# Second products of two more groups as seven products of sums, block 0's result summed in the output by transfers, and weights paced by a modelled clock

## The chip, the cores and the metric

The kernel runs on one core of a Trainium2 chip. Its engines work side by side, each in its own order: TensorE (PE, matmuls; PEld is its loading of weights), VectorE (DVE), ScalarE (ACT), GpSimd (POOL) and SyncE (SP, which here only issues transfers). The metric is the device time of one execution in microseconds, lower is better. The kernel before was timed in three runs, and one more execution was profiled.

## The reference, cut to what matters

```python
x = retention(q, k, v)                      # [1536, 512], 2 sequences of 768, 8 heads of 64
xn = x / sqrt(mean(x * x) + 1e-6) * rms_g
x2 = (silu(xn @ w_gate) * (xn @ w_val)) @ w_out     # layer 1: 512 -> 1536 -> 512
h  = x2 @ w_in                                      # layer 2: 512 -> 2048 -> 512
out = maximum(0.01 * h, h) @ w_out2
```

The weights arrive as 64-bit floats. Every product is made of three float32r matmuls (high x high, high x low, low x high), so each operand has a high part (a ScalarE copy into float32r) and a low part (a VectorE difference).

## The kernel before

The 1536 tokens are three blocks of 512 (0, 1, 2). The hidden units are cut into blocks of 128: 12 in layer 1, 16 in layer 2. Four of these make a group: groups 0 to 2 are layer 1, groups 3 to 6 are layer 2. A group first makes its *first products* (g and v, or i) and then its *second products* (o, or p), which are summed over the four hidden blocks of the group in four PSUM banks and then added to a sum over groups in SBUF.

**First products.** Block 0 is computed plainly: `whole`, 12 matmuls of 128x512. Blocks 1 and 2, for a pair of hidden blocks, are made by `quad` as seven products of sums (the Strassen-Winograd scheme) of 6 matmuls each, in the order p1, p2, p6, p5, p7, p3, p4; p6, p5, p7 and p4 read T2, T1, T3 and T4, sums of the activations of blocks 1 and 2 that `sums_of` prepares once for each layer. At the border of the layers they are made from the last result of layer 1: VectorE sums (L773), ScalarE high parts (L776), VectorE low parts (L779).

**Second products.** `down` (12 matmuls) handles one hidden block and one token block. In the groups of `seven` (with `SEVEN = 2`: groups 5 and 6) only block 0 goes through `down`; blocks 1 and 2 go through `seventh`, seven products of sums for each pair of hidden blocks. That takes sums of pairs of weights p (L415, with parts L418 and L422, names w_sp), differences of activations in `follow` (L671), seven high and low parts for a pair instead of four, and after each of the seven products two additions of results (L722). `seventh` turns the result, so block 1 and 2 of layer 2 are kept turned in `y2` and turned back at the end. In these groups the second products of block 0 come one group later, between the first products.

**Weights.** A weight of 128x512 is fetched by SP as 64-bit words (three places, tag raw), taken apart by ScalarE (`prepare`, two copies), put together on VectorE (two small and two full-size operations: L456, L460, L465, L474), and split into a high part (ScalarE, L477) and a low part (VectorE, L481). The pieces are steps in the list `converting`. Finished weights lie in 14 places (12 of tag u, 2 of units2) until their last product.

**Order.** The start (all of the retention) follows an order written out by hand. Then `run` goes through the list of products that `plan` made: after each product it emits high parts of the next activations, up to two entries of `sums`, then `RATE` = 4 conversion steps for a full product (8 when behind, half for a half product), then low parts. `need` forces the conversion of a weight that is not there. The framework's scheduler may still move an instruction ahead of one that waits: the order on an engine is not always the program's.

**Result.** `evac2` copies (group 3, ScalarE, L743) or adds (groups 4 to 6, VectorE, L745) the four banks into `y2`, and in the last group sends block 0's rows out.

```python
        if gi in seven:
            for f in fs[::2]:
                own = [fill.pop(0) for _ in range(2)]
                for i7, (keys, step) in enumerate(quad("i", f)):
                    put(keys, step)
                    if i7 in BEHIND[2] and own:
                        own.pop(0)()
            wholes = [...]
            for n, more in zip((1, 5, 6, 3, 7, 2, 4), (1, 0, 1, 0, 1, 0, 1)):
                for f in fs[::2]:
                    ...   # seventh(gi, n, f)
                if more:
                    wholes.pop(0)()
```

Of the kernel before, what the change touches and what calls it, by code (L numbers as in the profile page):

```python
# [27 lines left out]
RATE = 4.0  # L28
TWICE = "gvi"
SEVEN = 2  # L30
# [29 lines left out]
def chain_kernel(ctx: ExitStack, tc: tile.TileContext, qk_t, kv, w1, w2, mask, qdec, kdec, sdec, rms_g, ident, out):  # L60
# [427 lines left out]
    def queue(unit):  # L488
        key, after, ops = unit
        take = lambda names: [ops.pop(n) for n in names if n in ops]  # L490
        if key in index and dict(wq)[key] is None:
            converting.extend(tails + take("123H4h"))
            tails[:] = take("Ll")
            return
        converting.extend(take("P12"))
        if after is not None and ("P" in opened_units[after][2] if after in opened_units else True):
            converting.append(lambda: prepare(after))
        converting.extend(tails + take("34H"))
        tails[:] = take("L")
# [29 lines left out]

    def convert(n=1):  # L530
        for _ in range(n):
            if not converting and not start_unit():
                converting.extend(tails)
                tails.clear()
                if not converting:
                    return
            converting.pop(0)()

    def need(key):
        while key not in wt:  # L540
            if not converting and not start_unit():
                assert tails
                converting.extend(tails)
                tails.clear()
            converting.pop(0)()
# [41 lines left out]
    def upper(key):  # L587
        if key in made:
            x = made.pop(key)
            h = gp.tile([P, 512], F32R, tag="gh", name="g{}_{}_{}h".format(*key))  # L590
            nc.scalar.activation(out=h, in_=x, func=AF.Copy)
            halves[key] = x, h

    def lower(key):
        if key in halves:
            x, h = halves.pop(key)
            l = gp.tile([P, 512], F32R, tag="gl", name="g{}_{}_{}l".format(*key))
            nc.vector.tensor_tensor(out=l, in0=x, in1=h.bitcast(F32), op=ALU.subtract)
            parted[key] = h, l
            if key[0] == "q":  # L600
                follow(key[1], key[2])

# [20 lines left out]
    def evac1(gi, b, banks):  # L623
# [13 lines left out]
        if last:  # L637
            def high(m):
                nc.scalar.activation(out=x2h[b][:, m, :], in_=acc[b][:, m, :], func=AF.Copy)

            def low(m):
                nc.vector.tensor_tensor(
                    out=x2l[b][:, m, :], in0=acc[b][:, m, :], in1=x2h[b][:, m, :].bitcast(F32), op=ALU.subtract
                )

            for do in (high, low):
                sums.extend([lambda m=m, do=do: do(m) for m in own])
            if b == 2:
                one, two = slice(0, 2), slice(2, 4)
                sums.extend(in_pairs(sums_of(acc, x2h, x2l, acc[1][:, one], acc[1][:, two], x2h[2][:, one], x2l[2][:, one])))  # L650
# [14 lines left out]
    turns = {}  # L665

# [19 lines left out]
    def seventh(gi, n, f):  # L686
        fs = groups[gi][1]
        key = ("q", f, n)
        if n == 1 and f == fs[0]:
            gather(gi)  # L690
        upper(key)
# [31 lines left out]
        if gi == len(groups) - 1 and LAST[b, row] == n:  # L723
            t = units.tile([P, 2, 16, 32], F32, tag="u", name=f"turned{b}_{row}")
            for m in range(2):
                nc.vector.transpose(
                    out=t[:, m], in_=y2[b][:, 2 * row + m, :].rearrange("p (j r) -> p j r", r=32)
                )
                for i in range(4):
                    o = (2 * row + m) * P + i * 32  # L730
                    nc.sync.dma_start(
                        out=out[offs[b]:offs[b] + 512, o:o + 32].rearrange("(j r) d -> r j d", r=32),
                        in_=t[32 * i:32 * i + 32, m],
                    )

    def evac2(gi, b, banks):
        first, last = gi == len(G1), gi == len(groups) - 1
        if first:
            y2[b] = xp.tile([P, 4, 512], F32, tag=f"acc{b}", name=f"y2acc{b}")
        for m in range(4):  # L740
            dst = y2[b][:, m, :]
            if first:
                nc.scalar.activation(out=dst, in_=banks[m], func=AF.Copy)  # L743
            else:
                nc.vector.tensor_tensor(out=dst, in0=banks[m], in1=dst, op=ALU.add)  # L745
            if last:
                r0 = offs[b] + m * P
                nc.sync.dma_start(out=out[r0:r0 + P, :], in_=dst)
# [5 lines left out]
    def sums_of(x, xh, xl, t1, t4, h1, l1):  # L754
# [58 lines left out]
    def place(n, key, own=None):  # L813

        if n == "v":
            return gates.pop(key)
        return scratch(f"{n}{key[0]}_{key[1]}") if own is None else own
# [23 lines left out]

    def whole(n, f, b, h, l):
# [3 lines left out]
        consume(n, f, b)  # L846
# [13 lines left out]
    def quad(n, f):  # L860
# [5 lines left out]
        def kept_sum(m, src):  # L866
            q[m] = scratch(f"{n}{m}_{f}")
            nc.scalar.activation(out=q[m], in_=src, func=AF.Copy)

        def added(key, src, m):  # L870
            t = q.pop(m)
            a = place(n, key, t)
            mid = t if n == "v" else a
            nc.vector.tensor_tensor(out=mid, in0=src, in1=t, op=ALU.add)
            use[n](key, mid, a)
# [33 lines left out]
        def p4():  # L909
            half(q["X"], own[1], True, "T4", False)  # L910
            use[n]((e, 1), q["X"], place(n, (e, 1)))
# [5 lines left out]
    def plan():  # L917
# [12 lines left out]
        for gi, (kinds, fs) in enumerate(groups):  # L930
# [18 lines left out]
            first = gi == len(G1)  # L949
            if gi in seven:  # L950
                for f in fs[::2]:
                    own = [fill.pop(0) for _ in range(2)]
# [4 lines left out]
                wholes = [lambda f=f: put((f"i{f}",), lambda: whole("i", f, 0, h, l)) for f in fs]  # L957
                for n, more in zip((1, 5, 6, 3, 7, 2, 4), (1, 0, 1, 0, 1, 0, 1)):
# [4 lines left out]
                    if more:  # L963
                        wholes.pop(0)()
                continue
            if first:

                for f, d in zip(fs, fill):
                    d()
                    put((f"i{f}",), lambda f=f: whole("i", f, 0, x2h, x2l))  # L970
# [134 lines left out]
    owed = 0.0  # L1105
# [12 lines left out]

    for i, (keys, b, step) in enumerate(steps[FIXED:], FIXED):
        ahead = max([index[k] for ks, _, _ in steps[i + 1:i + 4] for k in ks[:1] if k in index], default=0)  # L1120
        run(i, keys, b, step, RATE if started[0] > ahead else 2 * RATE)
# [69 lines left out]
```

## Time and profile before

| what | value |
|---|---|
| median of three runs | 587.68 us (587.67 to 588.03) |
| profiled execution, its own time | 587.79 us |
| span of the profiled execution | 586.0 us |
| TensorE, VectorE, ScalarE, GpSimd busy | 577.4, 480.8, 343.9, 19.3 us |
| granted TensorE clock, mean | 1.000 |

The span runs from the first to the last instruction; the execution's own time is 1.8 us longer. Busy time counts the time in which an engine has at least one instruction at work. Matmuls overlap: one is listed at 389 ns, but twelve of them take 2.72 us. VectorE's instructions overlap a little at their ends too.

### The profile page before, as it was taken

Reading aid. Unit: us, or ns where it says so; the run is one execution under the profiler, and the core shown is the slowest. Engines: PE = TensorE matmul, PEld = TensorE weight load, DVE = VectorE, ACT = ScalarE, POOL = GpSimd, SP = SyncE. Lnnn points to the kernel's source line nnn. Section 1 sums busy time; section 2 is a strip of 40 time slices with the busy share of each in tenths; the row PEclk is TensorE's granted clock in tenths of the full one; section 3 lists DMA queues with packets and bytes.
Section 4 is the critical chain, followed back from the end, with each engine's and each line's share of the span. In section 5 each row is a group of like instructions: output and inputs, shape, how many; then the busy total and the mean of one; then the engine's idle time right before and its main releaser. Section 6 shows DMA issues by size and latency. Waiting matters only on the chain.

```text
span 586.0 us, 8323 instructions
## 1 busy us (share of the span) xinstructions
PE 577.4 (99%) x3131; PEld 476.3 (81%) x3131; DVE 480.8 (82%) x865; ACT 343.9 (59%) x624; POOL 19.3 (3%) x20
## 2 busy tenths in 40 slices
PE   8899999999999999999999999999999999999997
PEld 6788788888888888888888888888888888888885
DVE  5899999999768589598598988874777679997893
ACT  2789656777655455365574666876653564574430
POOL 2332100000000000000000000000000000000000
PEclk9999999999999999999999999999999999999999
DMA  8991240534223023123230220422211010210055
GB/s 335 407 390 44 73 143 1 155 98 115 66 78 108 31 72 108 37 73 110 70 107 1 70 76 0 144 72 73 72 37 36 30 43 3 70 37 0 1 89 127
DMA packets 31769, 52.77 MB, mean 90 GB/s; under 512 B 18929, under 2 KB 19057, under 8 KB 31729
## 3 DMA queue, kind: packets, MB, share of 16 engines
q1 hardware_dynamic: 31584, 52.24, 27.7%
q8 instruction: 24, 0.39, 0.3%
q14 instruction: 17, 0.13, 0.1%
q10 hardware_dynamic: 144, 0.00, 0.0%
HBM read 49.09 MB, written 3.15 MB: 89 GB/s over the span
## 4 chain that ended last, share of the span: by engine, by line
PE 87%; DMA 6%; DVE 3%; ACT 2%; issue 1%; SPq 0%; POOLq 0%; DVEq 0%; ACTq 0%
PE ao L583 17%; PE ap L583 15%; PE iX L855 7%; PE i L554 7%; PE v L554 6%; PE g L554 6%; PE vX L855 5%; PE gX L855 5%; PE X L703 4%; PE iZ L855 4%; PE Z L703 3%; PE vZ L855 2%; PE gZ L855 2%; DMA qkv<-in_qk_t 2%; PE iY L855 2%; DMA qkv<-in_kv 2%
## 5 line engine op out<-in xcount | busy, mean ns | idle before, releaser
L583 PE MATMUL ap<-w_p,gp_0h 128*128 128x512 f32 x128 | 39.4, 389 | 0.0
L554 PE MATMUL g<-xh,w_g 128*128 128x512 f32 x128 | 31.8, 390 | 0.0
L554 PE MATMUL v<-xh,w_v 128*128 128x512 f32 x128 | 31.7, 390 | 0.0
L554 PE MATMUL i<-x2h,w_i 128*128 128x512 f32 x128 | 31.6, 389 | 0.0
L583 PE MATMUL ao<-go_2h,w_o 128*128 128x512 f32 x96 | 31.5, 389 | 0.0
L583 PE MATMUL ao<-go_0h,w_o 128*128 128x512 f32 x96 | 31.5, 389 | 0.0
L583 PE MATMUL ao<-go_1h,w_o 128*128 128x512 f32 x96 | 30.5, 389 | 0.0
L554 PEld LDWEIGHTS g<-xh,w_g 128*128 128x128 f32 x128 | 23.9, 188 | 5.2 <-issue 0.2
L583 PEld LDWEIGHTS ap<-w_p,gp_0h 128*128 128x128 f32 x128 | 24.0, 188 | 5.0
L554 PEld LDWEIGHTS i<-x2h,w_i 128*128 128x128 f32 x128 | 24.0, 188 | 5.0
L554 PEld LDWEIGHTS v<-xh,w_v 128*128 128x128 f32 x128 | 23.9, 188 | 5.0
L583 PE MATMUL ap<-w_p,gp_0l 128*128 128x512 f32 x64 | 24.9, 389 | 0.0
L583 PEld LDWEIGHTS ao<-go_2h,w_o 128*128 128x128 f32 x96 | 18.0, 188 | 3.7
L583 PEld LDWEIGHTS ao<-go_1h,w_o 128*128 128x128 f32 x96 | 18.0, 188 | 3.7
L583 PEld LDWEIGHTS ao<-go_0h,w_o 128*128 128x128 f32 x96 | 18.0, 188 | 3.7
L583 PE MATMUL ap<-gp_2h,w_p 128*128 128x512 f32 x64 | 21.0, 389 | 0.0
L798 ACT ACTIVATE i<-i 128x512 f32<-128x512 f32 x16 | 9.6, 597 | 18.8 <-PE i L554 18.8
L583 PE MATMUL ap<-gp_1h,w_p 128*128 128x512 f32 x64 | 20.5, 389 | 0.0
L855 PE MATMUL iX<-th,w_si 128*128 128x512 f32 x64 | 19.7, 390 | 0.0
L855 PE MATMUL iZ<-x2h,w_si 128*128 128x512 f32 x64 | 19.7, 389 | 0.0
L583 PE MATMUL ao<-go_0l,w_o 128*128 128x512 f32 x48 | 18.7, 389 | 0.0
L583 PE MATMUL ao<-go_1l,w_o 128*128 128x512 f32 x48 | 18.7, 389 | 0.0
(303 smaller groups left out, 1662.7 us busy)
## 6 DMA issues: line engine op xcount, KB each, us to landing
raw_i<-in_w SPq DMA_DIRECT2D x16, 512.0 KB, 3.7
raw_p<-in_w SPq DMA_DIRECT2D x16, 512.0 KB, 3.6
raw_g<-in_w SPq DMA_DIRECT2D x12, 512.0 KB, 3.7
raw_v<-in_w SPq DMA_DIRECT2D x12, 512.0 KB, 3.7
raw_o<-in_w SPq DMA_DIRECT2D x12, 512.0 KB, 4.2
qkT<-in_qk_t SPq DMA_DIRECT2D x7, 512.0 KB, 6.5
kv<-in_kv SPq DMA_DIRECT2D x7, 512.0 KB, 8.0
qkv<-in_qk_t SPq DMA_DIRECT2D x5, 512.0 KB, 11.0
```

The lines of the kernel that those rows point to most:

```text
L554: nc.tensor.matmul(out=dst, lhsT=lhs, rhs=rhs, start=(n == 0), stop=(n == len(pairs) - 1), skip_group_check=True)
L583: nc.tensor.matmul(out=acc["b"][m], lhsT=lhs, rhs=rhs, start=(start and n == 0), stop=(stop and n == 2))
L703: nc.tensor.matmul(out=acc[side][m], lhsT=lhs, rhs=rhs, start=(start and f == fs[0] and k == 0), stop=(f == fs[-2] and k == 2), skip_group ...
L798: nc.scalar.activation(out=a, in_=x, func=AF.Prelu, alpha=0.01)
L855: nc.tensor.matmul(out=dst, lhsT=lhs, rhs=rhs, start=(start and n == 0), stop=(n == 5), skip_group_check=True)
```

## The change

`SEVEN` becomes 4: all four groups of layer 2 make the second products of blocks 1 and 2 by `seventh`. So the weights p of groups 3 and 4 are summed in pairs as well, and their activations are taken through `follow`.

Block 0's sum no longer lies in SBUF. In group 3 `evac2` copies the banks (ScalarE) into a tile `more` and SP writes it to the output; in groups 4 and 5 it is copied likewise and a transfer on POOL's queue adds it to the output in memory; in group 6 `recall` reads the output back into the tiles of raw weights, VectorE adds the last banks, and SP writes the rows. `more` lies where block 0's layer 1 sum was. It also holds block 0's activations of the first products (`place`), and at the border T2 for a while (`spare`), and the order of T1 to T4 and their parts changes.

At the border the plan begins with four `down`, then block 0's first product 0 (`HEAD`), and then the `quad`s follow; the other three products of block 0 come among the `seventh`s.

In `run` the low parts now follow the high parts directly. Conversion steps are emitted as long as each fits, by costs written in the code, below a modelled clock of TensorE (1.5 us more when behind); and the evacuations of a product (`later`) come after them, in `flush`. Results that are first in their place are copied by ScalarE (`fresh`).

```diff
-RATE = 4.0
-SEVEN = 2
+HEAD = "dddd0"
+OVER = 1.5
+COST = {n: ("a", 1.2) if n == "P" else ("a", 0.54) if n == "H" else ("v", 0.34 if n in "12" else 0.6) for n in "P1234HL"}
+COST_SUM = {n: ("a", 0.54) if n in "Hh" else ("v", 0.34 if n in "1234" else 0.6) for n in "123H4hLl"}
+SEVEN = 4
...
+    def convert_next():
+        key, engine, cost, do = converting.pop(0)
+        do()
+        done[key] = spend(engine, cost, done.get(key, 0.0))
...
         if f == fs[-1]:
-            (evac1 if L == "o" else evac2)(gi, b, acc.pop("b"))
+            banks = acc.pop("b")
+            first = gi in (0, len(G1))
+            by_copy = first or L == "p" and b == 0 and gi < len(groups) - 1
+            later.append(("a" if by_copy else "v", 2.4, lambda: (evac1 if L == "o" else evac2)(gi, b, banks)))
...
-            for do in (high, low):
-                sums.extend([lambda m=m, do=do: do(m) for m in own])
+            highs, lows = ([lambda m=m, do=do: do(m) for m in own] for do in (high, low))
             if b == 2:
                 one, two = slice(0, 2), slice(2, 4)
-                sums.extend(in_pairs(sums_of(acc, x2h, x2l, acc[1][:, one], acc[1][:, two], x2h[2][:, one], x2l[2][:, one])))
+                ops = sums_of(
+                    acc, x2h, x2l, acc[1][:, one], acc[1][:, two], x2h[2][:, one], x2l[2][:, one], extra()[:, two]
+                )
+                first_of = [lambda i=i: [ops[n]() for n in (f"{i}", f"h{i}")] for i in range(4)]
+                sums.extend(first_of[:2] + [ops["l1"]] + highs + [ops["l0"]] + lows)
+                sums.extend([first_of[2], ops["l2"], first_of[3], ops["l3"]])
+            else:
+                sums.extend(highs + lows)
...
+        if n == 5 and f == fs[0] and gi == len(groups) - 1:
+            recall()
...
-        for m in range(2):
-            dst = y2[b][:, 2 * row + m, :]
-            nc.vector.tensor_tensor(out=dst, in0=acc[side][m], in1=dst, op=ALU.add)
+        fresh = gi == len(G1) and (b, row) not in touched
+        touched.add((b, row))
...
+                if fresh:
+                    nc.scalar.activation(out=dst, in_=banks[m], func=AF.Copy)
+                else:
+                    nc.vector.tensor_tensor(out=dst, in0=banks[m], in1=dst, op=ALU.add)
...
         for m in range(4):
+            dst = y2[b][:, m, :] if b else more[0][:, m, :]
+            rows = out[offs[b] + m * P:offs[b] + (m + 1) * P, :]
+            if b and not first:
+                nc.vector.tensor_tensor(out=dst, in0=banks[m], in1=dst, op=ALU.add)
+            elif last:
+                nc.vector.tensor_tensor(out=partial[m], in0=banks[m], in1=partial[m], op=ALU.add)
+                nc.sync.dma_start(out=rows, in_=partial[m])
+            else:
                 nc.scalar.activation(out=dst, in_=banks[m], func=AF.Copy)
+                if not b and first:
+                    nc.sync.dma_start(out=rows, in_=dst)
+                elif not b:
+                    nc.gpsimd.dma_start(out=rows, in_=dst, accum_op=ALU.add)
...
+    def recall():
+        for m in range(0, 4, 2):
+            t = raws.tile([P, 2, 512], F32, tag="raw", name=f"partial{m}")
+            for k in range(2):
+                partial[m + k] = t[:, k]
+                nc.sync.dma_start(out=t[:, k], in_=out[offs[0] + (m + k) * P:offs[0] + (m + k + 1) * P, :])
...
+        s2 = t2 if spare is None else spare
         terms = [
             (t1, t3, c[:, one], h1, l1),
             (t3, t2, t3, th[:, 2:4], tl[:, 2:4]),
-            (t2, t2, t1, th[:, 0:2], tl[:, 0:2]),
-            (t4, c[:, two], t2, th[:, 4:6], tl[:, 4:6]),
+            (s2, t2, t1, th[:, 0:2], tl[:, 0:2]),
+            (t4, c[:, two], s2, th[:, 4:6], tl[:, 4:6]),
         ]
+        if spare is not None:
+            terms[1:3] = terms[2:0:-1]
...
+            if first:
+                for n in HEAD:
+                    if n == "d":
+                        fill.pop(0)()
+                    else:
+                        f = fs[int(n)]
+                        put((f"i{f}",), lambda f=f: whole("i", f, 0, x2h, x2l))
...
-    def run(i, keys, b, step, rate):
-        nonlocal owed
+    def flush():
+        for engine, cost, do in later:
+            do()
+            spend(engine, cost, clock["pe"])
+        later.clear()
+
+    def run(i, keys, b, step, behind):
         need(keys[0])
+        start = max(clock["pe"], done.get(keys[0], 0.0))
         step()
+        clock["pe"] = start + (1.36 if keys[-1] == "half" else 2.72)
         next_parts(upper)
+        next_parts(lower)
         for _ in range(min(len(sums), SUMS)):
             sums.pop(0)()
-        owed += rate * (0.5 if keys[-1] == "half" else 1.0)
-        convert(int(owed))
-        owed -= int(owed)
-        next_parts(lower)
+            spend("v", 1.13)
+            spend("a", 0.97)
+        limit = clock["pe"] + (OVER if behind else 0.0)
+        while upcoming():
+            key, engine, cost, _ = converting[0]
+            if max(clock[engine], done.get(key, 0.0)) + cost > limit:
+                break
+            convert_next()
+        flush()
```

## Rows read from the trace of the kernel before

**Rows 1.** The page: span, busy time of each engine, TensorE's granted clock by slice.

```profile
span 586.0 us, 8323 instructions
...
PE 577.4 (99%) x3131; PEld 476.3 (81%) x3131; DVE 480.8 (82%) x865; ACT 343.9 (59%) x624; POOL 19.3 (3%) x20
...
PEclk9999999999999999999999999999999999999999
```

**Rows 2.** The chain in order of time: start, us, what.

```profile
73.22 2.72 PE ao L583 x12
...
484.08 2.72 PE i L554 x12
...
489.52 2.81 PE X L703 x12
...
580.30 2.73 DVE y2acc L745 x4
```

**Rows 3.** Busy by stage: length, PE, PEld, DVE, ACT, POOL, clock, DMA, GB/s.

```profile
260.00:326.02 66.02, 66.02 (x292) 54.64 (x292) 54.85 (x98) 37.61 (x63) 0.00 (x0) 1.00 0.23 75
326.02:353.22 27.20, 27.20 (x121) 22.52 (x120) 24.51 (x40) 17.03 (x28) 0.00 (x0) 1.00 0.21 72
353.22:481.19 127.97, 127.97 (x565) 105.70 (x564) 93.65 (x166) 80.11 (x139) 0.00 (x0) 1.00 0.18 58
481.19:511.35 30.16, 30.16 (x134) 24.54 (x132) 29.74 (x54) 15.83 (x26) 0.00 (x0) 1.00 0.11 35
511.35:541.27 29.92, 29.92 (x134) 24.77 (x132) 25.62 (x51) 17.41 (x31) 0.00 (x0) 1.00 0.06 18
541.27:571.40 30.13, 30.13 (x134) 24.84 (x133) 26.41 (x45) 12.28 (x20) 0.00 (x0) 1.00 0.26 44
```

**Rows 4.** Waits of PE's weight loading, 326 to 583: total, times, longest us.

```profile
PEld X L703 <- DVE gq_6l L598: 0.4, 2, 0.2
```

**Rows 5.** Groups of instructions: busy us, mean ns of one, idle before.

```profile
L743 ACT ACTIVATE y2acc<-ap 128x512 f32<-128x512 f32 x12 | 6.4, 599 | 0.2
...
L422 DVE TENSOR_TENSOR w_sp<-wa_p,w_sp 128x512 fp32r<-128x512 f32 x8 | 5.4, 690 | 8.5 <-ACT w_sp L418 8.4
```

**Rows 6.** VectorE in order of time at the border and at 511 us.

```profile
345.19 1.22 DVE L773 TENSOR_TENSOR x2acc<-x2acc,x2acc 128x1024 f32<-128x1024 f32 x1
346.32 0.69 DVE L636 TENSOR_TENSOR x2acc<-ao,x2acc 128x512 f32<-128x512 f32 x1
346.92 0.69 DVE L642 TENSOR_TENSOR x2l<-x2acc,x2h 128x512 fp32r<-128x512 f32 x1
...
511.18 0.42 DVE L456 TENSOR_SCALAR wa_p<-wa_p 128x512 f32<-128x512 f32 x1
511.51 0.42 DVE L415 TENSOR_TENSOR wa_i<-wa_i,wa_i 128x256 f32<-128x256 f32 x1
```

**Rows 7.** TensorE in order of time at the border.

```profile
345.06 1.98 PE L554 MATMUL i<-x2h,w_i 128*128 128x512 f32 x8
...
355.94 0.62 PE L855 MATMUL iX<-th,w_si 128*128 128x512 f32 x2
356.39 0.62 PE L855 MATMUL iZ<-x2h,w_si 128*128 128x512 f32 x2
```

**Rows 8.** ScalarE in order of time at the border.

```profile
353.45 1.06 ACT L776 ACTIVATE th<-x2acc 128x1024 fp32r<-128x1024 f32 x1 [0.68 <-DVE x2acc L773]
```

**Rows 9.** Transfers: issuing queue, count, KB each, median us to landing.

```profile
raw_i<-in_w SPq DMA_DIRECT2D x16, 512.0 KB, 3.7
...
qkv<-in_qk_t SPq DMA_DIRECT2D x5, 512.0 KB, 11.0
...
out<-y2acc SPq DMA_DIRECT2D x4, 256.0 KB, 2.1
```

**Rows 10.** GpSimd in order of time.

```profile
18.44 1.27 POOL L168 TENSOR_TENSOR qs<-qkT,qdec_sb 128x512 f32<-128x512 f32 x1 [3.90 <-DMA qkT<-in_qk_t]
...
37.91 1.73 POOL L168 TENSOR_TENSOR qs<-qkT,qdec_sb 128x512 f32<-128x512 f32 x1
```

More of the change, by code (lines that the diff above doesn't have):

```diff
@@ L489, in queue @@
         key, after, ops = unit
-        take = lambda names: [ops.pop(n) for n in names if n in ops]
+        cost = COST_SUM if dict(wq)[key] is None else COST
+        take = lambda names: [(key, *cost[n], ops.pop(n)) for n in names if n in ops]
         if key in index and dict(wq)[key] is None:
@@ L528, in prepare, with spend @@
         prepared[key] = a, m, high
+    clock = {"pe": 0.0, "v": 0.0, "a": 0.0}
+    done = {}
+    later = []
+    def spend(engine, cost, start=0.0):
+        clock[engine] = max(clock[engine], start) + cost
+        return clock[engine]
     def convert(n=1):
@@ L719, in seventh @@
             return
-        for m in range(2):
-            dst = y2[b][:, 2 * row + m, :]
-            nc.vector.tensor_tensor(out=dst, in0=acc[side][m], in1=dst, op=ALU.add)
-        if gi == len(groups) - 1 and LAST[b, row] == n:
-            t = units.tile([P, 2, 16, 32], F32, tag="u", name=f"turned{b}_{row}")
-            for m in range(2):
[L726 to L733, printed above, removed]
-                    )
+        banks = acc[side]
@@ new lines, in seventh, with put @@
+        fresh = gi == len(G1) and (b, row) not in touched
+        touched.add((b, row))
+        if b not in y2:
+            y2[b] = xp.tile([P, 4, 512], F32, tag=f"acc{b}", name=f"y2acc{b}")
+        def put():
+            for m in range(2):
+                dst = y2[b][:, 2 * row + m, :]
+                if fresh:
+                    nc.scalar.activation(out=dst, in_=banks[m], func=AF.Copy)
+                else:
+                    nc.vector.tensor_tensor(out=dst, in0=banks[m], in1=dst, op=ALU.add)
+            if gi == len(groups) - 1 and LAST[b, row] == n:
+                t = units.tile([P, 2, 16, 32], F32, tag="u", name=f"turned{b}_{row}")
+                for m in range(2):
+                    nc.vector.transpose(
+                        out=t[:, m], in_=y2[b][:, 2 * row + m, :].rearrange("p (j r) -> p j r", r=32)
+                    )
+                    for i in range(4):
+                        o = (2 * row + m) * P + i * 32
+                        nc.sync.dma_start(
+                            out=out[offs[b]:offs[b] + 512, o:o + 32].rearrange("(j r) d -> r j d", r=32),
+                            in_=t[32 * i:32 * i + 32, m],
+                        )
@@ L816, in place @@
             return gates.pop(key)
+        if n == "i" and key[1] == 0:
+            return extra()[:, key[0] % 4, :]
         return scratch(f"{n}{key[0]}_{key[1]}") if own is None else own
@@ L840, in consume, with consume_later @@
         use[n]((f, b), x, place(n, (f, b)))
+    def consume_later(n, f, b):
+        later.append(("v" if n == "v" else "a", 0.62 if n == "v" else 0.52, lambda: consume(n, f, b)))
     def whole(n, f, b, h, l):
@@ L866, in kept_sum, with put @@
         def kept_sum(m, src):
-            q[m] = scratch(f"{n}{m}_{f}")
-            nc.scalar.activation(out=q[m], in_=src, func=AF.Copy)
+            def put():
+                q[m] = scratch(f"{n}{m}_{f}")
+                nc.scalar.activation(out=q[m], in_=src, func=AF.Copy)
+            later.append(("a", 0.52, put))
         def added(key, src, m):
[L871 to L875, printed above, removed]
+            def put():
+                t = q.pop(m)
+                a = place(n, key, t)
+                mid = t if n == "v" else a
+                nc.vector.tensor_tensor(out=mid, in0=src, in1=t, op=ALU.add)
+                use[n](key, mid, a)
+            later.append(("v", 1.2 if n == "v" else 0.6, put))
         def p1():
@@ L910, in p4 @@
             half(q["X"], own[1], True, "T4", False)
-            use[n]((e, 1), q["X"], place(n, (e, 1)))
+            later.append(("v" if n == "v" else "a", 0.6, lambda: use[n]((e, 1), q["X"], place(n, (e, 1)))))
             used(own[1])
@@ L956, in plan @@
                             own.pop(0)()
-                wholes = [lambda f=f: put((f"i{f}",), lambda: whole("i", f, 0, h, l)) for f in fs]
+                wholes = [lambda f=f: put((f"i{f}",), lambda: whole("i", f, 0, h, l)) for k, f in enumerate(fs) if not first or str(k) not in HEAD]
                 for n, more in zip((1, 5, 6, 3, 7, 2, 4), (1, 0, 1, 0, 1, 0, 1)):
@@ L962, in plan @@
                         put(keys, lambda n=n, f=f, gi=gi: seventh(gi, n, f))
-                    if more:
+                    if more and wholes:
                         wholes.pop(0)()
```

48 lines of the change are left out of this document (25 added, 23 removed).

## The prediction

> **What bounds the kernel now.** I read the page first, then the chain in order of time, then busy time by stage, then groups of instructions and single stretches. The page says that TensorE is busy 99% of the span and VectorE 82%, at a granted clock of full speed (2.4 GHz) in every slice [rows 1]. A busy share of pipelined matmuls could hide slack, so the chain is the better witness: from about 75 us on it is made almost wholly of TensorE pieces, and a piece of 12 matmuls takes 2.72 us wherever nothing disturbs it, which is 0.2267 us for each matmul [rows 2]. Only the end is different: 2.73 us of VectorE sums and the last transfers [rows 2]. So the time is start + matmuls x 0.2267 us + what TensorE waits + tail, and every matmul that goes is worth 0.2267 us as long as the other engines keep up. Whether they do is the whole question. By stage [rows 3], VectorE is busy 24.51 + 93.65 + 29.74 + 25.62 + 26.41 = 199.9 us of the 245.4 us from 326.02 (the last four output products of layer 1) to 571.40 (the last four of layer 2). The reader should look at 481.19 to 511.35 above all: the stage of the seven products in the third group of layer 2. There VectorE is busy 98.6%, and TensorE still loses only 30.16 - 29.92 = 0.24 us, in waits for the low parts of the sums [rows 4].
>
> **Matmuls removed.** A group of four hidden blocks costs 3 token blocks x 4 x 4 x 3 = 144 matmuls in its second products when computed plainly. As seven products it costs 48 for block 0 plus 2 pairs x 7 x 2 x 3 = 84, so 132. Two groups change: 24 matmuls fewer, 24 x 0.2267 = **-5.44 us**. Nothing else on TensorE changes in number: the first products were seven-product sums in all four groups already.
>
> **VectorE work added.** Per pair of hidden blocks in the two groups (four pairs): four 128x256 sums of weights and two low parts for the new weights, four differences of activations in `follow`, and three more low parts (7 instead of 4). That is 16 small and 36 full-size operations. Result sums: the plain groups had 4 full sums each for three blocks in group 4 and copies on ScalarE in group 3. Now group 3 has 6 sums (three of its seven results come second into their place; the other four are copies) and group 4 has 14; group 5 loses block 0's four, group 6 keeps them. Counted from the code, lines 722 and 745 go from 28 + 20 to 48 + 4, so +4. In all 16 small and 40 full-size operations. A full-size one is listed at 0.69 us, but back to back they start 0.60 us apart, and small ones 0.33 us apart [rows 5, 6]. The bounds are 16 x 0.33 + 40 x 0.60 = 29.3 us and 16 x 0.42 + 40 x 0.69 = 34.3 us. ScalarE gets 8 + 12 high parts and 8 more copies of results, 28 x 0.60 = 17 us [rows 5]; at 59% of the span [rows 1] it has room.
>
> VectorE then has 229 to 234 us of work in 245.4 - 5.4 = 240 us: 96 to 98%. It was 66.02 - 54.85 = 11.2 us idle between 260 and 326 us [rows 3], where the first weights of layer 2 are made, so some of it can go earlier, as far as the 14 places for weights allow. For the steady state I count one whole cycle (seven-product stage of one group and first products of the next, 264 matmuls, 59.85 us): 8 weights of 2 small and 3 full-size operations 19.7, 4 pairs of weight sums 10.1, 14 + 4 low parts 10.8, 8 differences 4.8, 14 result sums 8.4, 6 sums of first products 3.6: 57.4 us, or 96%. It fits with 2.4 us to spare, and the stage at 98.6% shows that TensorE hardly suffers at such a share. I therefore put the added work at **0 us**; its cover is VectorE's idle time, and if VectorE cannot be kept that full, each per cent missed costs about 0.6 us a cycle (rival B).
>
> **The seven-product stages.** The two that exist lose 0.24 and 0.21 us [rows 3, 4]. Two more: **+0.5 us** (0 if the low parts, which now stand ahead of the weight work in the order, come sooner).
>
> **The border between the layers.** Before, the four last `down` of layer 1 alternate with block 0's first products, and two more `down` of layer 2 follow: the last layer 1 piece ends at 345.06 and T2 is first needed at 355.94, 10.9 us later [rows 7]. With `HEAD` the four stand first and one product (2.72) and two halves (2.72) follow: T2 is needed after 5.44 us, T1 after 6.80, T3 after 8.16 (or 9.5, behind the half that needs only B22), T4 after 10.88. VectorE's part of that chain: T1 1.13, last result sum 0.60, T2 1.13, then ScalarE's high part 1.06, T2's low part 1.13 [rows 6, 8]: about 5.1 us plus hand-overs, in time by a hair. Then T1's low part 1.13, two low parts of B22 1.2, T3's sum, high and low part 3.3: about 10.8 us, late by 1.3 to 2.6 us. That the order can bend is seen before: iX<-th stops after two of its six matmuls, iZ goes between [rows 7]. Bounds 0 and 3 us, the latter with weight work in between; I take **+1.3 us**, in the lower half because the new order in `evac1` puts T2 and its low part first.
>
> **Block 0 through the output.** For groups 3 to 5 block 0's sums become ScalarE copies into `more`, four plain writes on SP's queue, eight accumulating transfers on POOL's queue, and four reads back in group 6. POOL has nothing else to do in layer 2, 0.00 us busy in every stage [rows 3]. SP has weight fetches behind the four writes; a fetch lands in 3.7 us [rows 9] and is asked for a whole weight ahead, so no term. No row shows an accumulating transfer. The nearest rows: 2.1 us for a plain write of the same 256 KB, 11.0 us for the slowest landing of any load [rows 9]. The place in `more` is wanted again by the next product of block 0, which ends 1.36 + 2.72 + 2.72 = 6.8 us after the last `down`. At 2.1 us it is hidden, at 11.0 us it would hold ScalarE 4.2 us in each of two groups. I take the near row, **0 us**. The Trainium skill ("DMA: Bandwidth & Descriptors", Anatomy of one DMA) gives about 2.0 us plus bytes over 436e3 us for such a transfer; an estimate from that page is 2.6 us for 256 KB, also hidden, and no run here has shown it yet. The final `down` still ends with four VectorE sums and four writes, so the tail stays as it is.
>
> **Sum.** -5.44 + 0.5 + 1.3 + 0 = -3.6 us. The profiled execution took 587.79 us for its 586.0 us span, 0.11 us above the median of the runs, 587.68. So 584.1 us there, and **584.0 us** against the median.
>
> **Rivals.** A is the above, TensorE stays the bound: chance 0.63, own range 581.8 (all waits gone) to 586.4.
>
> B, slower: VectorE sets the pace. For it: 96% needed, while the one whole cycle that the trace has (481.19 to 541.27) kept VectorE at only 55.36 / 60.08 = 92% [rows 3]. Against it: much of that idle time was waiting for TensorE when no weight was left to make. At 92% a cycle takes 57.4 / 0.92 = 62.4 us, 2.5 us more than TensorE's; two cycles (the one behind group 3 has 4.8 us fewer sums) and the border give 587.8 - 5.4 + 0.5 + 1.3 + 5.1 = 589.3 us; at 90%, 3.9 us a cycle, 592. It decides from about 93.5% downwards: 1.6 us lost in each of two cycles cancel the 3.6. Chance 0.17.
>
> C: the pacing makes weights too late. Before, each full product released 4 conversion steps, 8 when behind; now a step goes only if it fits under a modelled clock, else `need` forces it just before the product. The chain of one weight begun that late is 2 ScalarE copies, 2 small and 3 full-size VectorE operations and a high part: 1.2 + 0.8 + 2.1 + 0.6 = 4.7 us. One such weight in all gives 588.8 us, half of one 586.5. Against it: the modelled costs (0.34, 0.60) are those of rows 6. Chance 0.12.
>
> D: GpSimd's transfers disturb VectorE. A GpSimd operation that took 1.27 us alone took 1.73 us at 37.91 us, while VectorE was busy on two-input operations [rows 10], so the two do touch each other. If each of four transfers a cycle held VectorE for 1.27 us, 5.1 us would meet the 2.4 us spare: 2.7 us in two cycles, 584.1 + 5.4 = 589.5 us; with half of that, no loss. The Trainium skill ("SBUF — State Buffer", Who interferes with whom) says that the two share a port pair that one locks against the other, and that descriptors written by GpSimd meet VectorE's two-port modes. By that rule the small operations would be the ones held; the stretched row agrees that there is such a meeting, on GpSimd's side. Chance 0.08.
>
> **Chances.** 0.2% (1.2 us) is about what a measurement can tell from no change. Faster by more: A 0.63, C 0.03, D 0.02: 0.68. Within it (586.5 to 588.9): B 0.02, C 0.05, D 0.04: 0.11. Slower: B 0.15, C 0.04, D 0.02: 0.21. The range runs from A's lower end, 581.8, to 590.0, which takes in B at 92%, C and D, and leaves out B at lower shares.
>
> **What would show it.** Right: 24 matmuls fewer; pieces still 2.72 us; from the border on VectorE 94% or more; the first iX<-th after the last ao by 6 to 8 us with a wait of 1 to 2 us there; about 0.2 us lost in each of four seven-product stages; accumulating transfers landing within 6 us. Wrong: TensorE waits for w_i, w_si or w_sp (B if VectorE is full at that time, C if it is idle), ScalarE waiting for a transfer from `more`, or small VectorE operations well over 0.42 us while POOL works (D).

## The result

The changed kernel takes **583.05 us**, the median of four runs (582.67 to 583.39), against 587.77 us (587.67 to 588.03) for the kernel before: ratio 0.9919 [0.9902, 0.9936], so 4.7 us or 0.8% faster. The forecast was 584.0 us. The profiled execution took 583.3 us for a span of 581.3 us, 4.7 us less than the span before [rows 1].

The page of the changed kernel: span, busy time of each engine and number of its instructions, then the busy tenths of VectorE and the granted clock by slice.

```profile
span 581.3 us, 8448 instructions
...
PE 571.3 (98%) x3107; PEld 471.1 (81%) x3107; DVE 505.8 (87%) x921; ACT 355.9 (61%) x652; POOL 26.6 (5%) x28
...
DVE  4899999999578579697688999999999999997793
...
PEclk9999999999999999999999999999999999999999
```

Against [rows 1] TensorE has 3131 - 3107 = 24 matmuls fewer and VectorE 921 - 865 = 56 instructions more: both counts are the forecast's (24; 16 small and 40 full-size). VectorE's busy time rose by 25.0 us. TensorE still runs at full speed in every slice. The slices show where VectorE's new work lies: nines almost without a break in the second half.

Layer 2 of the changed kernel in eight stretches, the first from the last four `down` of layer 1. Columns: length, busy time of PE, PEld, DVE, ACT and POOL with their instructions, clock, DMA share, GB/s.

```profile
326.72:354.27 27.55, 27.55 (x120) 22.37 (x121) 27.07 (x41) 17.27 (x28) 0.00 (x0) 1.00 0.09 30
354.27:386.99 32.72, 32.72 (x146) 26.95 (x145) 32.51 (x62) 25.66 (x48) 0.00 (x0) 1.00 0.15 49
386.99:416.90 29.91, 29.91 (x133) 24.77 (x132) 29.91 (x59) 23.88 (x44) 0.00 (x0) 1.00 0.37 124
416.90:446.82 29.92, 29.92 (x133) 24.77 (x132) 29.66 (x55) 19.00 (x34) 0.00 (x0) 1.00 0.21 70
446.82:476.75 29.93, 29.93 (x134) 24.78 (x133) 29.69 (x60) 22.90 (x42) 2.28 (x3) 1.00 0.35 108
476.75:506.67 29.92, 29.92 (x134) 24.77 (x133) 29.38 (x53) 18.45 (x33) 1.45 (x2) 1.00 0.32 69
506.67:536.58 29.91, 29.91 (x133) 24.77 (x132) 25.86 (x52) 19.57 (x35) 2.15 (x3) 1.00 0.10 21
536.58:566.50 29.92, 29.92 (x133) 24.77 (x132) 24.67 (x41) 12.09 (x20) 1.34 (x2) 1.00 0.54 108
sum 239.78, PE 239.78 PEld 197.97 DVE 228.76 ACT 158.82 POOL 7.22; mean PE 29.97 PEld 24.75 DVE 28.59 ACT 19.85 POOL 0.90
```

This is the table to read. From 326.72 to 506.67 VectorE is busy 178.2 of 179.95 us, 99%. TensorE loses 0.42 us of that time at the border, in the first two stretches (60.27 us), and nothing behind it: a cycle of two stretches takes 59.83, 59.85 and 59.83 us, and 264 matmuls of 0.2267 us are 59.85. VectorE is at 99% in the first two of these three cycles; in the last it falls to 86 and 82%. In all 239.78 us, where the kernel before needed 245.24 us from the same point to its last four output products: **-5.46 us**, against -5.44 for 24 matmuls. That the two agree so closely is partly luck: 1080 and 1056 matmuls at 0.2267 us are 244.80 and 239.36 us, so the kernel before lost 0.44 us there (its two seven-product stages [rows 4]) and the changed one loses 0.42 (the border).

The chain shows the same: `seventh` pieces of 12 matmuls at the bare 2.72 us, where one of before took 2.81 [rows 2].

```profile
425.23 2.72 PE X L738 x12
...
485.07 2.72 PE X L738 x12
...
493.23 2.72 PE X L738 x12
```

Of the 5.46 us some 0.7 are missing in the span, and they are lost ahead of this stretch. The chain of this execution begins with a load of the mask that landed 0.85 us later than before, of which 0.4 us are left when the matmuls begin, and has 0.3 us without a named cause just before 326.72:

```profile
2.12 5.91 DMA mask_sb<-in_mask
...
326.59 0.13 issue
326.72 11.17 PE ao L603 x48
```

The late load is this execution's own, not the change's: a second copy of the same kernel (*after_again* below) has a span of 580.9 us and lands the same load after 5.01 us. The 0.3 us are there again in that copy, so they belong to the changed kernel; with the old pacing (*rate* below) they are not at this place.

### The profile page after: what moved, and what is told of

Read it like the earlier page. It is cut to its first block, busy times and chain, and to the rows that moved or that the text cites. A ratio compares the mean times of both kernels' runs of the same rounds, so it can differ in the third digit from the quotient of the medians.

```text
span 581.3 us, 8448 instructions
## 1 busy us (share of the span) xinstructions
PE 571.3 (98%) x3107; PEld 471.1 (81%) x3107; DVE 505.8 (87%) x921; ACT 355.9 (61%) x652; POOL 26.6 (5%) x28
## 4 chain that ended last, share of the span: by engine, by line
PE 88%; DMA 6%; DVE 3%; ACT 2%; issue 1%; SPq 0%; POOL 0%; DVEq 0%; POOLq 0%; ACTq 0%
PE ao L603 17%; PE iX L931 8%; PE ap L603 7%; PE X L738 7%; PE i L574 7%; PE v L574 7%; PE g L574 6%; PE Z L738 6%; PE vX L931 5%; PE gX L931 5%; PE iZ L931 4%; PE vZ L931 2%; PE gZ L931 2%; DMA qkv<-in_qk_t 2%; PE iY L931 2%; DMA qkv<-in_kv 2%
## 5 line engine op out<-in xcount | busy, mean ns | idle before, releaser
L800 POOL DMA_DIRECT2D out<-more x8 | 7.2, 1078 | 461.7 <-ACT more L796 461.5
L879 DVE TENSOR_TENSOR g<-v,g 128x512 f32<-128x512 f32 x16 | 10.9, 688 | 14.5 <-PE v L574 14.5
L869 ACT ACTIVATE more<-i 128x512 f32<-128x512 f32 x16 | 9.5, 594 | 21.5 <-PE i L574 21.5
L662 DVE TENSOR_TENSOR x2acc<-ao,x2acc 128x512 f32<-128x512 f32 x24 | 15.5, 686 | 4.1 <-PE ao L603 4.1
L603 PE MATMUL ao<-go_2l,w_o 128*128 128x512 f32 x48 | 18.7, 389 | 0.0
```

The source lines that it names most:

```text
L603: nc.tensor.matmul(out=acc["b"][m], lhsT=lhs, rhs=rhs, start=(start and n == 0), stop=(stop and n == 2))
L800: nc.gpsimd.dma_start(out=rows, in_=dst, accum_op=ALU.add)
L869: nc.scalar.activation(out=a, in_=x, func=AF.Prelu, alpha=0.01)
L879: nc.vector.tensor_tensor(out=a, in0=x, in1=a, op=ALU.mult)
```

## The experiments

They ran on three chips, each together with the kernel before, which took 587.73 to 587.78 us there; the changed kernel itself, run again on one of them as a control, took 582.89 us (582.74 to 583.15), 0.9918 [0.9904, 0.9931]. 

> The changed kernel itself once more, unaltered, as the measure for the three others on the same chip: 583.05 within 0.4 us.

### How much of the gain is the seven products: two, three and four groups

```diff
-HEAD = "dddd0"
+HEAD = "d0d1d2d3"
-SEVEN = 4
+SEVEN = 2      # seven2;  3 in seven3
```

With this HEAD the border's order is that of before. The sum T2 then overwrites two of block 0's activations in `more` in group 3, so block 0's output is not the reference's; no work is left out.

seven2: 

> The changed kernel with groups 3 and 4 plain, as before (two groups as seven products), the border alternating; block 0 still goes through the output and the weights are still paced by the modelled clock. By matmuls alone: 24 more, 5.44 us, so 588.1 to 588.6 us, the time of the kernel before or up to 0.5 us above. If the other two parts are worth something by themselves, it is clearly below 587.7: what it is below is theirs.

seven3: 

> The changed kernel with group 3's second products plain again (three groups as seven products) and the four last outputs of layer 1 alternating with block 0's first products, as before. If the gain is matmuls times 0.2267 us, 12 more matmuls cost 2.72 us and the alternating border gives back at most 0.4 us: 585.4 to 585.9 us. If the pacing or the new border made the gain, the time stays at 583 to 584 us. TensorE should show 3119 matmuls and no more waits than in the changed kernel.

| groups as seven products | us | ratio |
|---|---|---|
| 2 (seven2) | 588.81 (588.49 to 591.8) | 1.0021 [1.0011, 1.0032] |
| 3 (seven3) | 585.96 (585.86 to 586.28) | 0.997 [0.9958, 0.9982] |
| 4 (control, HEAD as changed) | 582.89 (582.74 to 583.15) | 0.9918 [0.9904, 0.9931] |

The first step is worth 2.85 us, the second 3.1 (with the border's order in it); 12 matmuls are 2.72. seven2 and seven3 each came out just above the upper end of what was expected. So the gain is the matmuls, and the other two parts of the change, block 0 through the output and the new pacing, are no gain alone: seven2 is 1.0 us slower than before. Its profiled execution has 0.6 us of that (span 586.6 us). The waits of PE's weight loading have changed places: those for gq_6l, gq_7l and gq_4l of the kernel before [rows 4] are gone, and these have come:

```profile
PEld iX L931 <- ACT is L945: 0.9, 2, 0.5
...
PEld ap L603 <- DVE gp_1l L619: 0.4, 1, 0.4
```

L945 is ScalarE's copy of a first product out of its bank. The changed `run` emits such copies (`later`) behind the weight steps; that this order causes the waits was not tested.

### How much VectorE time is left: three doses

The low part of weights of layer 2 is computed twice (result unchanged), or block 0's twelve copies out of PSUM go to VectorE.

```diff
 # extra_v: key[0] in "ip", 32 weights, +19.2 us;  extra_half: key[0] == "p", 16 weights, +9.6 us
-            v.tensor_tensor(out=u[:, 1, :], in0=a, in1=u[:, 0, :].bitcast(F32), op=ALU.subtract)
+            for _ in range(2 if key[0] in "ip" else 1):
+                v.tensor_tensor(out=u[:, 1, :], in0=a, in1=u[:, 0, :].bitcast(F32), op=ALU.subtract)
 # vec_copies: 12 copies, +7.2 us
-                nc.scalar.activation(out=dst, in_=banks[m], func=AF.Copy)
+                nc.vector.tensor_copy(dst, banks[m])
```

The modelled cost of that step is doubled with it, or moved to VectorE.

vec_copies: 

> The changed kernel with the evacuation of the plain second products' banks of block 0 (groups 3, 4 and 5, four each) copied by VectorE instead of ScalarE, which costs VectorE what the sums in SBUF of the kernel before cost it: 2.4 us a cycle. If VectorE is at its limit, 2 to 2.4 us for each of two to three groups: 587 to 590 us, and the way through the output is what pays for the added groups. If there are 2.4 us spare in each cycle, the copies take just these: 583 to 584 us.

extra_half: 

> Only the 16 weights of the second products get their low part twice: 9.6 us more of VectorE work. 7.2 us more (12 copies moved to VectorE) cost 0.65 us, 19.2 us more cost 10.2 us. If VectorE has a fixed amount to spare in layer 2, about 9 us, and everything beyond it is TensorE's wait, 0.6 to 2 us: 583.7 to 585 us. If each added microsecond costs the same 0.53 us from the first on, 5.1 us: 588.1 us.

extra_v: 

> The changed kernel with the low part of each of layer 2's 32 single weights computed twice by VectorE (the second writes the same values again), and the modelled clock told of it: 32 x 0.60 = 19.2 us more of VectorE work, 4.8 us for each cycle of 59.85 us. If VectorE is at its limit (99 per cent busy from 327 to 507 us), what does not fit into its idle time late in layer 2 (4 us) comes out as waits of TensorE: about 10 us, 593 us. If the count of the forecast is right (96 per cent needed, 2.4 us spare in each cycle), 2.4 us in two or three cycles: 588 to 590 us. If VectorE is only full because work is pulled forward and far from deciding, 583 to 585 us.

| kernel | VectorE work added | us | above the control |
|---|---|---|---|
| vec_copies | 7.2 us | 583.70 (583.59 to 583.94) | 0.8 |
| extra_half | 9.6 us | 584.84 (584.71 to 584.99) | 1.95 |
| extra_v | 19.2 us | 593.24 (591.08 to 594.27) | 10.35 |

What VectorE could take without cost is the work added minus the time lost: 6.4, 7.7 and 8.9 us. Between the second and the third dose 9.6 us of work cost 8.4 us. So there are some 6 to 9 us of room in layer 2 as a whole, and behind it most of each added microsecond comes out on TensorE: rival B's mechanism. The forecast's sum for the whole layer left 6 to 11 us. Its sum for one cycle (57.4 of 59.85 us used, 2.4 spare) fits less well: extra_v was expected at 588 to 590 us by that count and at 593 if VectorE was at its limit, and it took 593.24. The loss is not spread evenly either. In the stretches of extra_v (rows in the last section) the first three cycles together take 2.7 us more than in the changed kernel and the last one 8.0, so work done ahead pays for a while.

Not all of that is VectorE's. Waits of PE's weight loading in extra_v, then two waits of ScalarE, then TensorE in order of time:

```profile
PEld X L739 <- ACT w_sp L421: 3.6, 3, 3.0
PEld iX L932 <- ACT iu L946: 2.8, 5, 2.0
PEld X L739 <- DVE gq_4l L620: 1.0, 1, 1.0
```
```profile
ACT w_sp L421 <- DVE wa_p L418: 3.5, 4, 1.7
ACT wa_p L531 <- DMA raw_p<-in_w: 1.8, 1, 1.8
```
```profile
537.70 0.74 PE L932 MATMUL iX<-th,w_si 128*128 128x512 f32 x2 [1.57 <-ACT iu L946]
559.94 0.50 PE L739 MATMUL X<-gq_6h,w_sp 128*128 128x512 f32 x1 [2.54 <-ACT w_sp L421]
561.30 0.63 PE L739 MATMUL Z<-gq_5l,w_sp 128*128 128x512 f32 x1
```

The longest wait is VectorE's: ScalarE's high part of a sum of weights stood waiting for VectorE's sums. The one at 537.70 us stands behind a ScalarE that waited 1.8 us for the transfer of a weight. That transfer was issued at 527.5 us, 0.6 us behind an accumulating transfer of block 0, and landed after 7.9 us; another one, issued at 477.8 us and 0.5 us behind such a transfer, took 7.2, and the rest of this run's weights in layer 2 took 3.4 to 4.3. So the two kinds of transfer may hold each other up, which was not tested. And just behind the longest wait TensorE's clock was at its lower level (1.2 GHz) for 3.4 us, which cost about 1.6 us: matmuls started 0.43 us apart instead of 0.23. So the 8.4 us are more than VectorE's own share, and how sharp its limit is stays open. The modelled clock, told of the doubled cost, also releases the steps later; that was not separated from VectorE's time.

### Do the transfers of block 0 hold anything: each issued twice

```diff
                     nc.gpsimd.dma_start(out=rows, in_=dst, accum_op=ALU.add)
+                    nc.gpsimd.dma_start(out=rows, in_=dst, accum_op=ALU.add)
```

Groups 4 and 5 are then in block 0's output twice.

> The changed kernel with each of the eight accumulating transfers of block 0 issued twice, one behind the other (block 0's output then holds groups 4 and 5 twice). If a transfer on GpSimd's queue holds VectorE's small operations for about the 1.1 us that GpSimd needs for it, eight more cost up to 8.8 us of VectorE time where it is 99 per cent busy: 586 to 590 us, with small operations well over 0.42 us at 474 and 535 us. If they do not meet, 583.0 within 0.4 us, and the transfers are hidden twice over as long as the second lands before its place in SBUF is written again (6.8 us behind the last product).

585.30 us (585.13 to 585.6), 0.9959 [0.9944, 0.9974]: 2.4 us more than the control, between the two expectations. The doubled transfer waits for the first one to land, then ScalarE waits for the place in `more`, and the parts of a sum that ScalarE and VectorE make behind it (gq_6) are late for TensorE. ScalarE, GpSimd and the waits of PE's weight loading:

```profile
484.37 0.60 ACT L870 ACTIVATE more<-i 128x512 f32<-128x512 f32 x1 [3.75 <-DMA out<-more]
```
```profile
478.38 0.86 POOL L801 DMA_DIRECT2D out<-more  x1 [0.46 <-DMA out<-more]
...
481.98 0.86 POOL L801 DMA_DIRECT2D out<-more  x1 [0.42 <-DMA out<-more]
```
```profile
PEld X L738 <- DVE gq_6l L619: 1.8, 2, 1.2
```

In the changed kernel a transfer issued once lands in 5.7 us in the median, the plain write of the same 256 KB in 2.1. The eight differ: four go out within 2.5 us of each other, and the first of each four lands after 4.0 us, those behind it after 5.2 to 7.0. ScalarE's write into `more` waits for TensorE's product, not for the transfer:

```profile
out<-more POOLq DMA_DIRECT2D x8, 256.0 KB, 5.7
...
out<-more SPq DMA_DIRECT2D x4, 256.0 KB, 2.1
```
```profile
474.47 3.73 POOL L800 DMA_DIRECT2D out<-more  x4 [405.44 <-ACT more L796]
```
```profile
DMA to landing us min/median/max: 4.0/5.7/7.0
```
```profile
482.38 0.60 ACT L869 ACTIVATE more<-i 128x512 f32<-128x512 f32 x1 [1.50 <-PE i L574]
```

So the transfers are hidden. The place that is wanted first is that of the first transfer: issued at 474.47, it lands at 478.5, and the place is written at 482.38, with 3.9 us to spare (the forecast's 2.1 us left 4.7). The other three places are wanted 8 us and more later. In accum_twice the two transfers for that first place together end 10.1 us after the first is issued, and that is too late by about 2 us. The Trainium skill ("DMA: Bandwidth & Descriptors", Anatomy of one DMA) led to an estimate of 2.6 us; the trace's 4.0 to 7.0 decides: the fit is too short for an accumulating transfer here.

The kernel also tests rival D. While GpSimd issues the doubled transfers (481.98 to 482.84 above), a small VectorE operation runs beside it; its group's mean in the changed kernel is 420 ns:

```profile
481.93 0.43 DVE L459 TENSOR_SCALAR wa_i<-wa_i 128x512 f32<-128x512 f32 x1
482.27 0.69 DVE L704 TENSOR_TENSOR is<-i,is 128x512 f32<-128x512 f32 x1
482.87 0.43 DVE L463 TENSOR_SCALAR wa_i<-wa_i 128x512 int32<-128x512 int32 x1
```

Neither it nor the full-size one (0.69 us) is stretched. The third row begins when GpSimd's issue is over and is there for comparison. The same holds in the traces of the changed kernel and all its variants here, taken together: 64 VectorE operations of 128x256 beside such an issue took 422 ns in the mean, the others 420, and 136 full-size ones with two inputs 687 against 685; only six of the kind in the first row met an issue. The meeting that the Trainium skill describes ("SBUF — State Buffer", Who interferes with whom) is not seen at these places; the loss in this kernel is the wait for the place.

### The border: none, one or two of block 0's products

```diff
-HEAD = "dddd0"
+HEAD = "dddd"      # head_none;  "dddd01" in head01
```

head_none: 

> The changed kernel with none of block 0's first products between layer 1's last outputs and the first halves (it goes among the seven products, as the other three do): T2 is wanted 2.72 us after the last output instead of 5.44. The chain of T1 and T2 takes at least 1.13 + 1.13 + 1.06 + 1.13 = 4.45 us after the last result sum. If nothing can be moved into the gap, TensorE waits 2 us more, 585 us; if other halves of the second pair are moved ahead, as the changed kernel's trace shows for six halves, well under 1 us more.

head01: 

> The changed kernel with two of block 0's first products, not one, between layer 1's last outputs and the first seven-product halves: T2 is wanted 2.72 us later. If the changed kernel's small waits there (0.4 us in all between 326 and 365 us) come from the chain of T1 to T4, most of it goes: 582.6 to 582.8 us. If they are hand-overs of the rearranged matmuls, no change: 583.0. A cost of the forecast's size, 1.3 us, is not there to be won.

head_none takes 584.34 us (584.13 to 584.36), 0.9941 [0.9929, 0.9954], 1.45 above the control; head01 582.61 us (582.57 to 582.65), 0.9913 [0.9898, 0.9928], 0.3 below. head_none lies between its two expectations. Without a product in between, the first half that needs T1 finds its high part late, and that is the first of several small waits:

```profile
340.42 0.73 PE L931 MATMUL iZ<-x2h,w_si 128*128 128x512 f32 x2 [0.29 <-ACT x2h L847]
```

With one, as in the changed kernel, TensorE never stands still there for long, since the order puts halves whose sums are ready between the matmuls of those whose sums are not. After two matmuls with T2's high part (343.16 us), while its low part is made, come those of the half with T1 (343.69); ahead of T3 (from 347.88) come the first half of the second pair, which needs no sum (345.97), and the half with B22 (346.88):

```profile
343.16 0.69 PE L931 MATMUL iX<-th,w_si 128*128 128x512 f32 x2
343.69 0.62 PE L931 MATMUL iZ<-x2h,w_si 128*128 128x512 f32 x2
...
345.97 0.62 PE L931 MATMUL iX<-x2h,w_i 128*128 128x512 f32 x2
...
346.88 0.71 PE L931 MATMUL iZ<-x2h,w_si 128*128 128x512 f32 x2
```

The forecast worked with the order of one pair alone, half behind half. The 0.3 us of head01 are near what the runs scatter by and come from two chips, and combined with the old pacing they did not show again:

head01_rate (HEAD as in head01, pacing as in *rate*): 

> Two of block 0's first products at the border and the old pacing by count together. Each alone came out 0.4 and 0.1 us below the changed kernel. If both only remove or keep small waits at the border, together they stay at 582.4 to 582.8 us, at least 5 us below the kernel before, and the modelled clock has no part in the gain. If the old pacing needs the tighter border, 583 us or more.

582.99 us (582.14 to 583.52), 0.9918 [0.9904, 0.9932]: as the control. In its trace the border loses little, but a wait for a low part in a seven-product stage is back:

```profile
PEld X L738 <- DVE gq_7l L619: 0.6, 1, 0.6
```

### Pacing, and the order of the low parts

```diff
 # rate: the pacing of before
-        limit = clock["pe"] + (OVER if behind else 0.0)
-        while upcoming():
-            key, engine, cost, _ = converting[0]
-            if max(clock[engine], done.get(key, 0.0)) + cost > limit:
-                break
-            convert_next()
+        owed[0] += (8.0 if behind else 4.0) * (0.5 if keys[-1] == "half" else 1.0)
+        convert(int(owed[0]))
+        owed[0] -= int(owed[0])
 # low_late: next_parts(lower) behind the conversions again
-        next_parts(lower)
         ...
+        next_parts(lower)
```

rate: 

> The changed kernel with the old pacing: 4 conversion steps for a full product, 8 when behind, half for a half product. If VectorE's room (1 to 2 per cent left between 327 and 507 us) is only enough with steps placed where they fit, low parts come late and TensorE waits: 1 to 4 us more, 584 to 587 us, with waits for gq low parts or for w_si and w_sp. If the pacing is worth nothing, 583.0 within 0.4 us.

low_late: 

> The changed kernel with the low parts of the next activations emitted after the conversion steps again instead of directly after the high parts. If that order is what removed the 0.2 us that each seven-product stage lost before, four stages lose 0.2 us each: 583.8 us, with waits of TensorE for gq_6l, gq_7l and gq_4l as before. If the modelled pacing alone removed them, 583.0 and no such waits.

rate takes 582.92 us (582.90 to 582.93), 0.9917 [0.9901, 0.9934]; low_late 582.93 us (582.78 to 583.12), 0.9918 [0.9903, 0.9933]. Neither differs from the control. The modelled clock is worth nothing measurable here, for or against. And in neither do the waits for low parts in the seven-product stages [rows 4] come back, so neither part is needed by itself to keep them away. With head01 and the old pacing together one came back, as shown above; so the pacing may have a share in it.

## Why the prediction held, step by step

The direction, the likeliest case (A) and its range held; the time was forecast 0.95 us too long.

- **Matmuls removed, -5.44 us.** Right: 24 fewer, and 2.85 and 3.1 us for one group each (layer 2 is shorter by 5.46 us, but with two small terms in it that happen to cancel, below). TensorE stays the bound: its pieces are back to back at 0.2267 us a matmul.
- **VectorE work at 0 us.** Right, and for the reason given. 56 instructions came, they fit, and behind the border TensorE lost nothing beside a VectorE that was 99% busy. Over the whole stretch it is 228.76 of 239.78 us, 95%, where 94% or more was named as a sign of being right. VectorE's busy time rose by 25.0 us, less than the 29.3 of the lower bound; operations that stood apart before at their listed 0.69 us and now stand 0.60 apart may be why, which was not tested. The 99% is partly work pulled forward: in the last two stretches it falls to 86 and 82%. The doses show what the cover is: 6 to 9 us in the whole layer (the forecast's 229 to 234 of 240 us left 6 to 11). Rival B's reading of 92% as what VectorE can sustain falls; its mechanism stands, and it begins with the smallest dose (0.8 us). Its threshold was also added up wrongly: 3.6 us over two cycles are 1.8 in each, not 1.6, so it would decide from about 93%.
- **Seven-product stages, +0.5 us.** Wrong: -0.45. The two new stages lose nothing, and the 0.24 and 0.21 us of the two that existed are gone as well, which the forecast had left in. It named the possibility (low parts ahead of the weight work), but low_late undid that order and the waits stayed away, and so with *rate* and in seven2. What removed them was not isolated; the old pacing and the old order of low parts together, or the new order of sums and results, were not tried.
- **The border, +1.3 us.** Mis-sized: 0.42 us in the cycle that holds it. T2 is first read 5.4 us after the last output of layer 1, as worked out, without the wait of 1 to 2 us that was named as a sign. VectorE's chain was a little longer than worked out: T2's low part is made 6.6 us after that output and T3's 11.3, where 5.1 and 10.8 were forecast. But TensorE's order at the border was taken as that of the first pair, half behind half; in the trace other halves fill the wait, and T3 is first read after 10.2 us instead of 8.2 to 9.5. head_none shows that there is little slack left: one product less, and 1.45 us go.
- **Block 0 through the output, 0 us.** Right in the sum, wrong in the row that it took: the transfer that decides lands after 4.0 us and the eight after 5.7 in the median (within 6 us was the sign), not 2.1. The plain write was the wrong guide for the time, though the time was hidden all the same; two such transfers one behind the other cost 2.4 us.
- **Pacing, rival C.** Did not happen: no weight is late in the changed kernel. *rate* shows that the old pacing would not have been late either.
- **Rival D.** Not seen, with twice as many transfers too. Its row was weak: the GpSimd operation called alone (at 18.44 us) had a VectorE operation of 0.42 us beside it.

The two wrong terms were 0.95 and 0.9 us too high, 1.8 together: -5.44 - 0.45 + 0.42 = -5.47 us is what the stretch of layer 2 shows (-5.46), against the forecast's -3.6. Of these 1.8 us, 0.7 were lost again ahead of it: 0.4 by the load that came late in this execution and 0.3 just before the last four outputs of layer 1, for which the forecast had no term. That is how a forecast of -3.6 stands 1.1 us from the span's -4.7. What stays open, besides the waits that went, is why seven2 loses 1.0 us against before: its trace shows 0.6 of it and names waits for `is` and one low part, their cause was not sought.

## What to carry to other kernels

When one engine is the bound and its pieces stand back to back, cost a change by the pieces that go, and ask of each other engine only whether its work per cycle, counted at the pitch of back-to-back operations, fits in the bound's cycle. A count of 96% did fit, and added work began to cost time within the room that the count for the whole layer had left, so add up that work instead of asking how busy the engine looked before. Where something waits at a border, look which other pieces the order can put in between before the wait is written down as a loss.

## What the runs showed of the hardware

- VectorE ran 178.2 of 179.95 us, and in the part of that time behind the border (386.99 to 506.67) TensorE was never late: a second engine at 99% was no loss by itself here.
- An accumulating transfer of 256 KB on GpSimd's queue landed in 4.0 us as the first of four and in 5.2 to 7.0 behind others, a plain one on SP's in 2.1. GpSimd was busy some 0.9 us for each, without a stretched VectorE operation beside it.
- Two weight transfers of 512 KB in extra_v, issued 0.5 and 0.6 us behind an accumulating one, landed in 7.2 and 7.9 us, its others in 3.4 to 4.3; one in extra_half, 0.4 us behind, in 5.2. In the changed kernel none was issued while an accumulating one was under way.
- In extra_v the granted clock was 0.95 of full speed, a mean of its two levels (1.2 and 2.4 GHz), in the stretch in which TensorE had stood still for 2.54 us; from 561 to 564 us, just behind that wait, it was at 0.50. In the stretches ahead, with shorter waits (1.57 us at 537.70), it was 1.00. Columns as in the table of stretches:

```profile
326.00:508.60 182.60, 182.12 (x794) 147.53 (x793) 179.68 (x323) 122.80 (x213) 3.66 (x4) 1.00 0.23 67
508.60:541.96 33.36, 31.79 (x139) 25.48 (x138) 31.40 (x61) 22.15 (x40) 3.68 (x4) 1.00 0.48 111
541.96:576.46 34.50, 31.41 (x128) 24.43 (x127) 32.34 (x59) 14.75 (x25) 0.00 (x0) 0.95 0.18 38
...
561.00:564.00 3.00, 3.00 (x9) 2.35 (x8) 1.23 (x3) 0.33 (x1) 0.00 (x0) 0.50 0.02 5
```
